# Two token tiles by transposing DMA, a joint first v stage, and a new work order in a fused linear-attention and FFN kernel

## The chip, the cores and the metric

The kernel runs on one core of a Trainium2 chip. The metric is the device time of one execution in microseconds (us); below, "the profiled execution" is a single execution recorded by the hardware profiler, with a record for every instruction of every engine and for the DMA transfers. The engines are PE (matrix multiply), DVE (vector), ACT (scalar, activations), POOL (general) and SP (here it only issues DMAs). PE writes to PSUM, which is used as eight banks in four pairs; DVE and ACT read PSUM, POOL doesn't.

## The reference

For 2048 tokens x of width 640, the output mixes a linear attention A and a gated FFN B with a gate per token:

```python
qkv = x @ wqkv                                   # 32 heads of 20
pq = einsum("bhsd,hdf->bhsf", q, w_phi)
pk = einsum("bhsd,hdf->bhsf", k, w_phi)
phi_q = concat([softmax(pq), softmax(-pq)])      # 40 features per head
phi_k = concat([softmax(pk), softmax(-pk)])
kv = einsum("bhsf,bhsd->bhfd", phi_k, v)
z  = einsum("bhsf->bhf", phi_k)
num = einsum("bhqf,bhfd->bhqd", phi_q, kv)
den = einsum("bhqf,bhf->bhq", phi_q, z)[..., None] + 1e-6
a = (num / den) @ wo
b = (silu(x @ w_gate) * (x @ w_up)) @ w_down     # F = 1728
g = sigmoid((x * gate_w).sum(-1, keepdims=True))
out = g * a + (1 - g) * b
```

All inputs and the output are bfloat16.

## The kernel before

The tokens are 16 tiles of 128 (`NT`), and four blocks of 512 (`NB`) for the FFN. Nothing is scheduled at run time: the string `ORDER` lists short items, and a loop at the end of `_build` emits the instructions of each item in that order. Each engine then runs its own instructions strictly in the order in which they were emitted; a tracker (`_Tracker.run`) adds semaphore waits for data and buffer conflicts. Work thus runs ahead on an engine until an instruction has to wait, and everything behind it on that engine waits too.

The items, with the engines that they use:

- `H` warm-up matmuls of ones (`NWARM` of them each), `G` puts gate_w as a further column into the v weights (`wvg`).
- `X t` transposes token tile t on PE (five 128x128 transposes from `xs`), and DVE copies it to `xT`. Tiles below `NPE` are loaded plainly into `xs` for this; all others are loaded straight into `xT` by a transposing DMA on SP (`load_x`).
- `V t`: v of tile t, ten matmuls of 320 columns into one PSUM pair; ACT copies it to one of six buffers `v1r`, and the gate's column to `svec`.
- `W m`: transposes of a row chunk of wk (from `wkn`), copied by DVE to `wT`; `Y` builds block-diagonal w_phi in `wbd` (two pieces on DVE, three on POOL); `M m` and `R m` multiply wk and wq with it ahead of time (wq is loaded transposed into `wTq`), copied to `wqk` by DVE (even m of `M`) or ACT.
- `K t`: ten matmuls, two exponentials on ACT into one of four `ekr`, sums and reciprocals on DVE, scaling on POOL. `E t`: eleven small matmuls that add tile t to kv in PSUM pair 3. `I` takes that pair out of the ring of pairs (`ring["n"]` from 4 to 3), `N` finishes kv on DVE and gives it back, `Z` broadcasts z.
- `Q t`: ten matmuls, two exponentials on ACT into one of three `eq`. `A t` (qsum), `B t` (qden) and `C t` (qscale) are DVE work of about 1.5, 1.5 and 3 us; `C` ends with a multiplication on POOL into `ph` and a transposing DMA on SP into `phiT`.
- `F b.k`: column chunk k of gate and up for block b: ten matmuls of 512 columns into one pair, tanh and copy on ACT, one DVE operation, one POOL multiplication into `hT`.
- `O b.p`: a third of the attention output of block b, copied by ACT to `oT`. `D b.u`: the last projection of a token tile, 38 matmuls of 320 columns, one scaling on ACT into `osb`, and the store to HBM, issued by SP. The very last tile is done in two halves of 19 matmuls, each with its own ACT operation and store.

Every item that needs PSUM takes the next pair in the ring (`next_pair`), so PE waits where the pair's last user (by four, or between `I` and `N` three, takings ago) has not been read out.

Before the loop, the loads are issued. On ACT's queue: gate_w, wv chunks 0, 2 and 4, x2, w_phi. On SP's queue: x0, wv chunks 1 and 3, x1, x3, five chunks of wk, x4 to x6 by transposing DMA, five chunks of wq by transposing DMA, x7 to x15 by transposing DMA. The item `L` then puts the FFN and output weights behind these on SP's queue.

All matmuls are emitted by the helper at L284, PE transposes by L296, ACT operations by L302, DVE and POOL operations by L308 (copies), L312, L316, L323 and L326, plain DMAs by L338 and transposing ones by L337.

Of the kernel before, what the change touches and what calls it, by code (L numbers as in the profile page):

```python
# [12 lines left out]
NT = S_TOK // P  # L13
NB = 4
NCH = 11
NPE = 4
NV = 6
NWARM = 3
FP = 120 * NCH
FK = FP + 8  # L20
ACTF = mybir.ActivationFunctionType
# [7 lines left out]


ORDER = """
L H0 H1 H2 G H3 H4 H5 X0 H6 H7 V0 X1 X2 X3 V1 Y W0 W1 W2 V2 W3 W4 V3 M0 M1 M2 M3 M4 K0 I V4 K1 R0
K2 V5 K3 E0 R2 V6 K4 E1 K5 R4 E2 K6 E3 V7 K7 R1 E4 V8 E5 K8 K9 V9 F0.0 V10 E6 K10 E7 F0.1 E8 V11
K11 E9 K12 V12 K13 R3 E10 K14 V13 E11 K15 Q0 V14 F0.2 V15 E12 E13 J E14 E15 N Q1 F0.3 Q2 A0 Z A1
B0 A2 F0.4 F0.5 F0.6 C0 B1 F0.7 F1.0 Q3 C1 A3 F0.8 F1.1 B2 F1.2 C2 F0.9 F0.10 B3 Q4 F1.3 A4 Q5 C3
F1.4 F0.11 T F0.12 B4 Q6 C4 A5 F1.5 F1.6 B5 F1.7 O0.0 A6 O0.1 F1.8 B6 Q7 A7 F0.13 O0.2 C5 F1.9
F1.10 Q8 C6 A8 B7 D0.0 D0.1 D0.2 Q9 F1.11 C7 D0.3 F2.0 F2.1 F2.2 F1.12 B8 O1.0 O1.1 O1.2 A9 C8
Q10 F2.3 F1.13 Q11 A10 F2.4 B9 F2.5 C9 A11 B10 Q12 D1.0 F2.6 C10 F2.7 D1.1 F2.8 B11 F2.9 F2.10
Q13 A12 C11 D1.2 Q14 D1.3 O2.0 A13 B12 A14 F3.0 B13 F3.1 F3.2 O2.1 C12 C13 F3.3 F3.4 B14 F2.11
Q15 F2.12 A15 F3.5 F2.13 C14 F3.6 O2.2 B15 F3.7 C15 F3.8 D2.0 F3.9 F3.10 F3.11 F3.12 D2.1 O3.0  # L40
O3.1 O3.2 F3.13 D2.2 D3.0 D3.1 D2.3 D3.2 D3.3
"""


# [143 lines left out]
def _build(nc, A_x, A_wqkv, A_w_phi, A_wo, B_x, B_w_gate, B_w_up, B_w_down, gate_w, out):  # L188
    tr = _Tracker(nc)
    pe, act, dve, pool, sp = nc.tensor, nc.scalar, nc.vector, nc.gpsimd, nc.sync  # L190
# [28 lines left out]
    omg = sb("omg", [P, NT], F32)  # L219
# [37 lines left out]
    wph = at("wph", [P, 5, DH], BF16, 28480)  # L257
# [17 lines left out]
    def mm(pairs):  # L275
        reads, writes = [], []
        for p in pairs:
            reads += [p[1], p[2]]
            writes.append(p[0])

        def fn():
            last = None
            for o, l, r, st, sp_, sk in pairs:
                last = pe.matmul(o, lhsT=l, rhs=r, start=st, stop=sp_, skip_group_check=sk)  # L284
            return last
        return run("pe", fn, list({id(a): a for a in reads}.values()), writes)
# [13 lines left out]
    def actop(o, i, func, scale=1.0):  # L300
        rd = [i] + ([scale] if isinstance(scale, bass.AP) else [])
        return run("act", lambda: act.activation(o, i, func, scale=scale), rd, [o])  # L302

    def copy(e, o, i):
        if e == "act":
            return actop(o, i, ACTF.Copy)
        eo = tr.eng[e]
        return run(e, lambda: eo.tensor_copy(o, i), [i], [o])  # L308
# [23 lines left out]
    def dma(e, dst, src, transpose=False):  # L332
        eo = tr.eng[e]

        def fn():
            if transpose:
                return eo.dma_start_transpose(dst, src)  # L337
            return eo.dma_start(dst, src)  # L338
        rd = [src] if src.tensor.name in tr.base else []
        wr = [dst] if dst.tensor.name in tr.base else []  # L340
        return run(e, fn, rd, wr, dma=True)
# [39 lines left out]
    H0 = [0, 6, 12, 19, 25]  # L381
    H1 = [7, 13, 20, 26, 32]
# [56 lines left out]
    def warm():  # L439

        pr = next_pair()
        mm([(bank(2 * pr, 0, P), ones[:, :], ones[:, :], True, True, False)] * NWARM)

    def vtile(t):
        pr = next_pair()
        pairs = [(bank(2 * pr + hb, 0, 320 + hb), xT[:, t, c, :], wvg[:, c, 320 * hb:640 + hb - 320 * (1 - hb)],
                  c == 0, c == 4, False) for c in range(5) for hb in range(2)]
        if t == 0:
            for c in range(5):
                mm(pairs[2 * c:2 * c + 2])  # L450
        else:
            mm(pairs)
        i = halves(pr).rearrange("p b (h d) -> p b h d", d=DH)
        o = v1v[:, t % NV, 0:H, 0:DH].rearrange("p (b h) d -> p b h d", b=2)
        copy("act", o, i)
        copy("act", svec[:, t:t + 1], bank(2 * pr + 1, 320, 321))

    def head_exps(pr, dst):
        i = halves(pr).rearrange("p b (h d) -> p b h d", d=DH)
        o = dst.rearrange("p (b h s d) -> p b h s d", b=2, s=2, d=DH)  # L460
        actop(o[:, :, :, 0, :], i, ACTF.Exp, 1.0)
        actop(o[:, :, :, 1, :], i, ACTF.Exp, -1.0)
# [183 lines left out]
    out_evs = []  # L646

    def ditem(bt, u):
        buf = bt % 2
        t = 4 * bt + u  # L650
        pr = next_pair()
        tok = slice(P * u, P * u + P)
        ls = [(hT[:, buf, k, tok], wd[:, k, :]) for k in range(13)]
        ls += [(hT[0:104, buf, 13, tok], wd[0:104, 13, :])]
        ls += [(oT[:, buf, m, tok], wog[:, m, :]) for m in range(5)]
        n = len(ls)
        half = [[(bank(2 * pr + hb, 0, 320), l, r[:, 320 * hb:320 * hb + 320], i == 0, i == n - 1, False)
                 for i, (l, r) in enumerate(ls)] for hb in range(2)]
        o = osb[:, t % 4, :]
        if t < NT - 1:  # L660
            mm([p for ab in zip(*half) for p in ab])
            actop(o.rearrange("p (b c) -> p b c", b=2), halves(pr), ACTF.Copy, omg[:, t:t + 1])
            out_evs.append(dma("sp", out2[t * P:(t + 1) * P, :], o))
            return
        for hb in range(2):
            mm(half[hb])
            c = slice(320 * hb, 320 * hb + 320)
            actop(o[:, c], bank(2 * pr + hb, 0, 320), ACTF.Copy, omg[:, t:t + 1])
            out_evs.append(dma("sp", out2[t * P:(t + 1) * P, c], o[:, c]))


    def kv_begin():
# [2 lines left out]
    def kv_end():  # L675
        kv_finish()
        ring["n"] = 4

    ops = {
        "H": lambda i: warm(), "X": xpose, "G": gcol, "V": vtile, "W": wxpose,  # L680
        "M": lambda m: premult(1, m), "R": lambda m: premult(0, m),
        "K": ktile, "E": kvtile, "L": load_ffn_weights, "T": tail_weights, "J": gates,
        "Y": w_blocks, "I": kv_begin, "N": kv_end, "Z": z_broadcast,
        "Q": qtile, "A": qsum, "B": qden, "C": qscale,
        "F": fitem, "O": oitem, "D": ditem,
    }
    for w in ORDER.split():
# [50 lines left out]
```

## Time and profile before

| | |
|---|---|
| median of 4 runs | 295.9 us (295.81 to 296.99) |
| profiled execution, its own time | 295.62 us |
| profiled execution, span from first to last instruction | 293.8 us |
| mean granted TensorE clock | 1.000 |
| DVE, ACT, POOL busy in the span | 171.7, 148.7, 158.0 us |
| DMA moved in the span | 21.28 MB |

The span is shorter than the execution's own time because that has work around the program's first and last instruction. "Busy" of PE counts a matmul from its start to its modelled end, and matmuls overlap, so starts of successive items are a better measure of their cost than the lengths. In the lists of groups, `out<-in` names the tile written and the tiles read; in timelines, a bracket tells how long the engine had been idle and what released it. The costliest groups of PE are the FFN's matmuls of 512 columns (520 of them, mean 379 ns from start to modelled end) and the last projection's of 320 columns (448 with `wd`, mean 299 ns). The page's chain of work that ended last is PE for 90% of the span, DVE for 5% and DMA for 2%.

Some durations that are used below: the DVE reductions of A and C take 1.48 us, the multiplication of B 1.45, the FFN's DVE operation 0.68, its tanh on ACT 0.60 and its copy 0.59; POOL's multiplications take 1.27 (FFN), 2.46 (`ph`) and 2.36 (`ekr`); the two exponentials of a K or Q tile take 1.41 together; a transposing DMA into `phiT` landed 3.5 us after its issue (3.5 to 4.0), one of x 2.9 to 5.5, wk chunks 5.2 to 5.5.

### The profile page before, as it was taken

Reading aid. Unit: us, or ns where it says so; the run is one execution under the profiler, and the core shown is the slowest. Engines: PE = TensorE matmul, PEld = TensorE weight load, DVE = VectorE, ACT = ScalarE, POOL = GpSimd, SP = SyncE. Lnnn points to the kernel's source line nnn. Section 1 sums busy time; section 2 is a strip of 40 time slices with the busy share of each in tenths; the row PEclk is TensorE's granted clock in tenths of the full one; section 3 lists DMA queues with packets and bytes.
Section 4 is the critical chain, followed back from the end, with each engine's and each line's share of the span. In section 5 each row is a group of like instructions: output and inputs, shape, how many; then the busy total and the mean of one; then the engine's idle time right before and its main releaser. Section 6 shows DMA issues by size and latency. Waiting matters only on the chain.

```text
span 293.8 us, 4908 instructions
## 1 busy us (share of the span) xinstructions
PE 288.1 (98%) x1981; PEld 174.2 (59%) x1981; DVE 171.7 (58%) x250; ACT 148.7 (51%) x252; POOL 158.0 (54%) x118
## 2 busy tenths in 40 slices
PE   7999999999999999999999999999999999999996
PEld 5777766766454544457764456647544455657774
DVE  2567874576979989997042777539269893100000
ACT  2278865775746665852235862353356644262112
POOL 8709887794268878855025384544056976410000
PEclk9999999999999999999999999999999999999999
DMA  7968799510002222204203021130302223000101
GB/s 228 197 114 113 213 358 362 116 23 0 2 0 49 51 49 49 49 2 82 63 22 73 3 49 29 44 71 2 94 0 49 51 49 71 3 22 25 45 22 48
DMA packets 45993, 21.28 MB, mean 72 GB/s; under 512 B 35794, under 2 KB 45970, under 8 KB 45970
## 3 DMA queue, kind: packets, MB, share of 16 engines
q1 hardware_dynamic: 44728, 20.27, 29.3%
q10 hardware_dynamic: 1242, 0.68, 0.8%
q8 instruction: 16, 0.26, 0.4%
q14 instruction: 7, 0.06, 0.1%
HBM read 9.78 MB, written 2.62 MB: 42 GB/s over the span
## 4 chain that ended last, share of the span: by engine, by line
PE 90%; DVE 5%; DMA 2%; ACTq 1%; ACT 1%; issue 0%
PE ps L284 90%; DMA xs<-in_A_x_dram 2%; DVE qw L323 1%; DVE hT L316 1%; PE ps L296 1%; ACTq L338 1%; DVE qw L316 1%; DVE qm L583 1%; DVE qz L323 0%; DVE ez L312 0%; ACT hT L302 0%; DVE qd L326 0%; DVE qc L588 0%; DVE qd L312 0%; ACT osb L302 0%
## 5 line engine op out<-in xcount | busy, mean ns | idle before, releaser
L312 POOL TENSOR_TENSOR hT<-hT,us 128x512 bf16<-128x512 bf16 (+1 forms) x56 | 69.8, 1259 | 62.5 <-DVE hT L316 62.4
L316 DVE SCALAR_TENSOR_TENSOR hT<-hT,ps 128x512 bf16<-128x512 bf16 (+1 forms) x56 | 37.6, 682 | 61.7 <-ACT hT L302 51.0
L284 PE MATMUL ps<-xT,wg 128*128 128x512 bf16 x260 | 64.6, 379 | 0.3 <-DVE hT L316 0.2
L284 PE MATMUL ps<-xT,wu 128*128 128x512 bf16 x260 | 64.6, 379 | 0.0
L284 PE MATMUL ps<-wd,hT 128*128 128x320 bf16 x448 | 63.7, 299 | 0.0
L302 ACT ACTIVATE hT<-ps 128x512 bf16<-128x512 f32 (+2 forms) x60 | 35.8, 596 | 47.0 <-PE ps L284 45.1
L284 PEld LDWEIGHTS ps<-wd,hT 128*128 128x128 bf16 x448 | 43.8, 98 | 17.8
L312 POOL TENSOR_TENSOR ph<-eq,qc 128x1320 bf16<-128x1320 bf16 x16 | 39.3, 2457 | 27.1 <-DVE qc L588 27.1
L284 PE MATMUL ps<-wqk,xT 128*128 128x320 bf16 x320 | 48.4, 299 | 0.1
L312 POOL TENSOR_TENSOR ekr<-ekr,krec 128x1280 bf16<-128x1280 bf16 x16 | 37.3, 2357 | 15.7 <-DVE krec L326 13.5
L284 PEld LDWEIGHTS ps<-xT,wu 128*128 128x128 bf16 x260 | 25.4, 98 | 30.7
L302 ACT ACTIVATE osb<-ps,omg 128x640 bf16<-128x640 f32 (+1 forms) x17 | 13.0, 762 | 58.5 <-PE ps L284 58.5
L284 PEld LDWEIGHTS ps<-xT,wg 128*128 128x128 bf16 x260 | 24.9, 98 | 29.5 <-issue 1.2
L284 PEld LDWEIGHTS ps<-wqk,xT 128*128 128x128 bf16 x320 | 30.4, 98 | 14.0 <-ACT us L302 0.5
L302 ACT ACTIVATE us<-ps 128x512 bf16<-128x512 f32 (+1 forms) x56 | 33.2, 593 | 0.6 <-POOL hT L312 0.5
L323 DVE TENSOR_REDUCE ksum<-ekr 128x64 f32<-128x1280 bf16 x16 | 23.5, 1468 | 14.7 <-ACT ekr L302 14.7
L302 ACT ACTIVATE eq<-ps 128x640 bf16<-128x640 f32 x32 | 22.5, 704 | 15.7 <-POOL ph L312 11.3
L302 ACT ACTIVATE ekr<-ps 128x640 bf16<-128x640 f32 x32 | 22.5, 704 | 8.4 <-PE ps L284 7.9
L284 PE MATMUL ps<-wvg,xT 128*128 128x320 bf16 (+1 forms) x160 | 24.8, 300 | 0.2 <-DMA wvg<-in_A_wqkv_dram 0.2
L284 PE MATMUL ps<-wog,oT 128*128 128x320 bf16 x160 | 24.5, 299 | 0.0
L323 DVE TENSOR_REDUCE qz<-eq 128x64 f32<-128x1280 bf16 x16 | 23.6, 1479 | 1.3 <-ACT eq L302 1.3
L323 DVE TENSOR_REDUCE qw<-ez 128x64 f32<-128x1280 bf16 x16 | 23.6, 1477 | 0.0
(71 smaller groups left out, 196.2 us busy)
## 6 DMA issues: line engine op xcount, KB each, us to landing
out_dram<-osb SPq DMA_DIRECT2D x15, 160.0 KB, 1.8
wd<-in_B_w_down_dram SPq DMA_DIRECT2D x1, 2080.0 KB, 16.6
wkn<-in_A_wqkv_dram SPq DMA_DIRECT2D x5, 160.0 KB, 5.4
wg<-in_B_w_gate_dram SPq DMA_DIRECT2D x1, 800.0 KB, 9.7
wu<-in_B_w_up_dram SPq DMA_DIRECT2D x1, 800.0 KB, 11.3
wog<-in_A_wo_dram SPq DMA_DIRECT2D x2, 375.0 KB, 6.6
wg<-in_B_w_gate_dram SPq DMA_DIRECT2D x1, 720.0 KB, 12.1
wu<-in_B_w_up_dram SPq DMA_DIRECT2D x1, 720.0 KB, 12.5
```

What stands on the lines that cost most here:

```text
L284: last = pe.matmul(o, lhsT=l, rhs=r, start=st, stop=sp_, skip_group_check=sk)
L296: last = pe.transpose(o, i, ident[0:k, 0:k])
L302: return run("act", lambda: act.activation(o, i, func, scale=scale), rd, [o])
L312: return run(e, lambda: eo.tensor_tensor(o, a, b, op), [a, b], [o])
L316: return run("dve", lambda: dve.scalar_tensor_tensor(out=o, in0=a, scalar=s, in1=b, op0=op0, op1=op1), rd, [o])
L323: return run("dve", lambda: dve.tensor_reduce(o, i, AX.X, ALU.add), [i], [o])
L338: return eo.dma_start(dst, src)
L583: run("dve", lambda: dve.tensor_tensor(v2(qm[:, s, :]), v2(qw[:, s, :]), qs, ALU.mult), [qw[:, s, :], qz[:, b, :]], [qm[:, s, :]])
```

## The change

- `NPE` goes from 4 to 2: tiles 2 and 3 are no longer loaded into `xs` and transposed on PE; they come by transposing DMA on SP like tiles 4 to 15.
- The loads are dealt out anew: x1 goes on ACT's queue ahead of its wv chunks; wv chunks 0, 2, 4 go on SP and 1, 3 on ACT; x2 and x3 by transposing DMA stand on SP behind the wv chunks and ahead of the five wk chunks.
- `U` (`vfirst`) replaces V0 and V1: it takes two PSUM pairs and runs both tiles chunk by chunk of wv; both are copied out afterwards.
- The second half of the last tile is stored by a DMA that ACT issues; the first half still by SP.
- `NWARM` is 4, with six `H` items ahead of everything instead of eight of 3 spread out.
- `ORDER` is another one throughout. The O items of a block now stand closer together, `I` stands before W4 instead of after K0, and the places of F, Q, A, B, C and D items among each other differ everywhere.

```diff
-NPE = 4
+NPE = 2
-NWARM = 3
+NWARM = 4
...
-L H0 H1 H2 G H3 H4 H5 X0 H6 H7 V0 X1 X2 X3 V1 Y W0 W1 W2 V2 W3 W4 V3 M0 M1 M2 M3 M4 K0 I V4 K1 R0
+H2 H0 H3 H1 L H5 H4 G X0 X1 U V2 W0 W1 Y V3 W2 W3 I W4 M2 M1 M0 M4 M3 K0 K1 K2 V4 K3 V5 R0 E0 V6
...
-B0 A2 F0.4 F0.5 F0.6 C0 B1 F0.7 F1.0 Q3 C1 A3 F0.8 F1.1 B2 F1.2 C2 F0.9 F0.10 B3 Q4 F1.3 A4 Q5 C3
-F1.4 F0.11 T F0.12 B4 Q6 C4 A5 F1.5 F1.6 B5 F1.7 O0.0 A6 O0.1 F1.8 B6 Q7 A7 F0.13 O0.2 C5 F1.9
...
-Q13 A12 C11 D1.2 Q14 D1.3 O2.0 A13 B12 A14 F3.0 B13 F3.1 F3.2 O2.1 C12 C13 F3.3 F3.4 B14 F2.11
-Q15 F2.12 A15 F3.5 F2.13 C14 F3.6 O2.2 B15 F3.7 C15 F3.8 D2.0 F3.9 F3.10 F3.11 F3.12 D2.1 O3.0
-O3.1 O3.2 F3.13 D2.2 D3.0 D3.1 D2.3 D3.2 D3.3
...
+F1.7 F0.11 A4 F1.8 Q5 Q6 F0.12 F0.13 F1.9 F1.10 A5 O0.0 B4 O0.1 O0.2 F1.11 B5 F1.12 C4 A6 Q7 B6
+D0.0 C5 A7 Q8 C6 D0.1 D0.2 B7 Q9 C7 A8 F1.13 D0.3 Q10 A9 B8 F2.0 C8 A10 O1.0 O1.1 B9 O1.2 F2.1
+F2.2 C9 Q11 B10 C10 D1.0 F2.3 Q12 A11 B11 D1.1 D1.2 Q13 F2.4 F2.5 A12 A13 F2.6 F2.7 F2.8 C11 F2.9
...
+F3.5 B15 F3.6 O2.1 O2.2 F3.7 F3.8 C14 D2.0 F3.9 D2.1 C15 F3.10 F3.11 F3.12 O3.0 O3.1 O3.2 F3.13
+D2.2 D2.3 D3.0 D3.1 D3.2 D3.3
...
     load_x(0)
+    load_x(1, "act")
     for c in range(5):
-        load_rows("sp" if c % 2 else "act", wvg[:, c, 0:D], c, 2 * D)
-    load_x(1)
-    load_x(2, "act")
+        load_rows("act" if c % 2 else "sp", wvg[:, c, 0:D], c, 2 * D)
+    load_x(2)
+    dma("act", wph[:, :, :], A_w_phi.rearrange("h e f -> (h e) f").rearrange("(c p) f -> p c f", p=P))
     load_x(3)
-    dma("act", wph[:, :, :], A_w_phi.rearrange("h e f -> (h e) f").rearrange("(c p) f -> p c f", p=P))
...
+    def vfirst():
+
+        prs = [next_pair(), next_pair()]
+        pairs = [v_pairs(t, prs[t]) for t in range(2)]
+        for c in range(5):
+            for t in range(2):
+                mm(pairs[t][2 * c:2 * c + 2])
+        for t in range(2):
+            v_out(t, prs[t])
...
-        for hb in range(2):
-            mm(half[hb])
-            c = slice(320 * hb, 320 * hb + 320)
-            actop(o[:, c], bank(2 * pr + hb, 0, 320), ACTF.Copy, omg[:, t:t + 1])
-            out_evs.append(dma("sp", out2[t * P:(t + 1) * P, c], o[:, c]))
+        mm(half[0])
+        actop(o[:, 0:320], bank(2 * pr, 0, 320), ACTF.Copy, omg[:, t:t + 1])
+        out_evs.append(dma("sp", out2[t * P:(t + 1) * P, 0:320], o[:, 0:320]))
+        mm(half[1])
+        actop(o[:, 320:D], bank(2 * pr + 1, 0, 320), ACTF.Copy, omg[:, t:t + 1])
+        out_evs.append(dma("act", out2[t * P:(t + 1) * P, 320:D], o[:, 320:D]))
```

`v_pairs` and `v_out` are the two halves of the old `vtile`: the ten matmuls of a tile, and ACT's two copies.

More of the change, by code (lines that the diff above doesn't have):

```diff
@@ L31 @@
 ORDER = """
-L H0 H1 H2 G H3 H4 H5 X0 H6 H7 V0 X1 X2 X3 V1 Y W0 W1 W2 V2 W3 W4 V3 M0 M1 M2 M3 M4 K0 I V4 K1 R0
-K2 V5 K3 E0 R2 V6 K4 E1 K5 R4 E2 K6 E3 V7 K7 R1 E4 V8 E5 K8 K9 V9 F0.0 V10 E6 K10 E7 F0.1 E8 V11
-K11 E9 K12 V12 K13 R3 E10 K14 V13 E11 K15 Q0 V14 F0.2 V15 E12 E13 J E14 E15 N Q1 F0.3 Q2 A0 Z A1
-B0 A2 F0.4 F0.5 F0.6 C0 B1 F0.7 F1.0 Q3 C1 A3 F0.8 F1.1 B2 F1.2 C2 F0.9 F0.10 B3 Q4 F1.3 A4 Q5 C3
-F1.4 F0.11 T F0.12 B4 Q6 C4 A5 F1.5 F1.6 B5 F1.7 O0.0 A6 O0.1 F1.8 B6 Q7 A7 F0.13 O0.2 C5 F1.9
-F1.10 Q8 C6 A8 B7 D0.0 D0.1 D0.2 Q9 F1.11 C7 D0.3 F2.0 F2.1 F2.2 F1.12 B8 O1.0 O1.1 O1.2 A9 C8
-Q10 F2.3 F1.13 Q11 A10 F2.4 B9 F2.5 C9 A11 B10 Q12 D1.0 F2.6 C10 F2.7 D1.1 F2.8 B11 F2.9 F2.10
-Q13 A12 C11 D1.2 Q14 D1.3 O2.0 A13 B12 A14 F3.0 B13 F3.1 F3.2 O2.1 C12 C13 F3.3 F3.4 B14 F2.11
-Q15 F2.12 A15 F3.5 F2.13 C14 F3.6 O2.2 B15 F3.7 C15 F3.8 D2.0 F3.9 F3.10 F3.11 F3.12 D2.1 O3.0
-O3.1 O3.2 F3.13 D2.2 D3.0 D3.1 D2.3 D3.2 D3.3
+H2 H0 H3 H1 L H5 H4 G X0 X1 U V2 W0 W1 Y V3 W2 W3 I W4 M2 M1 M0 M4 M3 K0 K1 K2 V4 K3 V5 R0 E0 V6
+E1 K4 V7 K5 R1 E2 K6 E3 V8 K7 V9 E4 V10 E5 K8 K9 E6 V11 E7 R3 K10 K11 R2 E8 F0.0 E9 V12 K12 K13
+F0.1 E10 V13 K14 E11 R4 F0.2 K15 V14 Q0 A0 V15 E12 F0.3 E13 E14 E15 N F1.0 Q1 A1 Z B0 F0.4 J Q2
+C0 F1.1 B1 F1.2 C1 F1.3 F0.5 A2 Q3 F0.6 F0.7 A3 B2 F0.8 F1.4 F0.9 B3 Q4 F0.10 T C2 F1.5 F1.6 C3
+F1.7 F0.11 A4 F1.8 Q5 Q6 F0.12 F0.13 F1.9 F1.10 A5 O0.0 B4 O0.1 O0.2 F1.11 B5 F1.12 C4 A6 Q7 B6
+D0.0 C5 A7 Q8 C6 D0.1 D0.2 B7 Q9 C7 A8 F1.13 D0.3 Q10 A9 B8 F2.0 C8 A10 O1.0 O1.1 B9 O1.2 F2.1
+F2.2 C9 Q11 B10 C10 D1.0 F2.3 Q12 A11 B11 D1.1 D1.2 Q13 F2.4 F2.5 A12 A13 F2.6 F2.7 F2.8 C11 F2.9
+D1.3 B12 C12 F2.10 F3.0 F2.11 B13 Q14 A14 F3.1 Q15 A15 F3.2 F2.12 B14 F3.3 O2.0 C13 F2.13 F3.4
+F3.5 B15 F3.6 O2.1 O2.2 F3.7 F3.8 C14 D2.0 F3.9 D2.1 C15 F3.10 F3.11 F3.12 O3.0 O3.1 O3.2 F3.13
+D2.2 D2.3 D3.0 D3.1 D3.2 D3.3
 """
@@ L442, in warm, with v_pairs, v_out @@
         mm([(bank(2 * pr, 0, P), ones[:, :], ones[:, :], True, True, False)] * NWARM)
[L444 to L452, printed above, removed]
+    def v_pairs(t, pr):
+        return [(bank(2 * pr + hb, 0, 320 + hb), xT[:, t, c, :], wvg[:, c, 320 * hb:640 + hb - 320 * (1 - hb)],
+                 c == 0, c == 4, False) for c in range(5) for hb in range(2)]
+    def v_out(t, pr):
         i = halves(pr).rearrange("p b (h d) -> p b h d", d=DH)
@@ L456, in vtile @@
         copy("act", svec[:, t:t + 1], bank(2 * pr + 1, 320, 321))
+    def vtile(t):
+        pr = next_pair()
+        mm(v_pairs(t, pr))
+        v_out(t, pr)
+    def vfirst():
[6 more added lines that the diff above has]
+            v_out(t, prs[t])
     def head_exps(pr, dst):
@@ L679, in _build @@
     ops = {
-        "H": lambda i: warm(), "X": xpose, "G": gcol, "V": vtile, "W": wxpose,
+        "H": lambda i: warm(), "X": xpose, "G": gcol, "U": vfirst, "V": vtile, "W": wxpose,
         "M": lambda m: premult(1, m), "R": lambda m: premult(0, m),
```

## The prediction

> **What bounds the kernel now.** I read the page first: the span, the busy times and the slices.
>
> ```profile
> span 293.8 us, 4908 instructions
> PE 288.1 (98%) x1981; PEld 174.2 (59%) x1981; DVE 171.7 (58%) x250; ACT 148.7 (51%) x252; POOL 158.0 (54%) x118
> PE   7999999999999999999999999999999999999996
> ```
>
> TensorE is busy for 288.1 of 293.8 us and only its first and last slices are not full. Nothing done to another engine can bring anything unless PE starts its dense stretch earlier, has less to do, stops less often on the way, or the tail behind it shrinks. 293.8 - 288.1 = 5.7 us is all the idle time there is. The list of PE's waits says where it lies:
>
> ```profile
> PE ps L284 <- DVE ones L330: 1.1, 1, 1.1
> PE ps L296 <- DMA xs<-in_A_x_dram: 0.9, 1, 0.9
> PE ps L284 <- DVE hT L316: 0.5, 2, 0.3
> ```
>
> 1.1 us is start-up, 0.9 us is the wait for x2 and x3, 0.5 us are two stops in the middle; 2.5 us more lie behind the last matmul. So I went to the timeline of PE's first 18 us, which the change rewrites (columns: start, length, engine):
>
> ```profile
> 4.20 0.85 PE L284 MATMUL ps<-ones 128*128 128x128 bf16 x6
> 5.00 1.29 PE L284 MATMUL ps<-wvg,xT 128*128 128x320 bf16 x8
> ...
> 6.73 0.44 PE L296 MATMUL ps<-ident,xs 128*128 128x128 bf16 x5
> 8.04 0.73 PE L296 MATMUL ps<-ident,xs 128*128 128x128 bf16 x10 [0.87 <-DMA xs<-in_A_x_dram]
> 8.61 1.54 PE L284 MATMUL ps<-wvg,xT 128*128 128x320 bf16 x10
> 9.99 1.00 PE L296 MATMUL ps<-ident,wkn 128*128 128x128 bf16 x15
> ```
>
> V0 begins at 5.00, X1 sits at 6.73, X2 and X3 come at 8.04 after the wait, V1 at 8.61. Starts give prices: a V tile 9.99 - 8.61 = 1.38 us (0.138 per matmul), a W item 1.02 / 3 = 0.34. The other engines' rows around it show what feeds this stretch and what ends it:
>
> ```profile
> 3.15 2.33 SPq L338 DMA_DIRECT2D wkn<-in_A_wqkv_dram  x5
> 5.52 4.70 SPq L337 DMA_TRANSPOSE xT<-in_A_x_dram  x3
> 11.45 1.27 POOL L312 TENSOR_TENSOR wbd<-wph,bmask 128x160 bf16<-128x160 bf16 x3
> 14.85 2.29 DVE L308 CAST wqk<-ps 128x640 bf16<-128x640 f32 x3 [1.08 <-PE ps L284]
> 17.19 0.11 PEld L284 LDWEIGHTS ps<-wqk,xT 128*128 128x128 bf16 x2 [0.22 <-DVE wqk L308]
> ```
>
> K0's last pair of matmuls waits for the third cast of wqk, so the preamble ends at 17.47, where the timeline has V4's first matmul. From there PE is dense. The point to forecast is when K0 ends in the new order, since both kernels have then done V0 to V3, all W and M items and K0.
>
> **The change, part by part: the front.** Removed are X2 and X3: ten transposes and two DVE copies; on PE they take 8.61 - 8.04 = 0.57 us, and the 0.87 us wait before them goes as a wait for a plain load. Warm-up stays at 24 matmuls (8x3 then, 6x4 now); back to back, at 0.103 each (9 from 2.74 to 3.67), they end near 3.6, so X0 stays where it was, at 3.67. X1 is new at this place: x1 is ACT's second issue at 1.41; ACT's issue at that time landed 2.9 us later, at 4.3. X1 then runs 4.3 to 4.8, its copy (0.49) ends near 5.45. U's first two matmuls go at 4.99, the rest from 5.45: 18 x 0.138 = 2.48, end 7.93. Its last chunk, c4, is the seventh load, as many as had landed before at 6.38 (issued 2.28, 4.1 to landing); U needs it at 7.4, a cover of 1 us. So V0 and V1 are done at 7.93, where before V1 ended at 9.99.
>
> V2 runs 7.93 to 9.31. x2 by transpose is SP's fifth issue, at about 2.65 (0.81, then four of 0.40 to 0.46). Transposes landed 2.9 to 5.5 us after issue, so by 8.15 at the latest: at worst 0.2 us late. x3 follows 1.3 to 2.2 us later, by 10.35 at worst; V3 wants it at 10.4.
>
> Now what is queued behind: wkn's five issues stand behind both transposes on SP. Three transposes took 4.70 us of SP, two take 3.1 to 3.4, so wkn starts near 6.0 instead of 3.15; x4 to x6, wTq, x7 to x15 and the FFN weights move back by 2.4 us (two transposes in, two plain issues out). Those later ones have cover: V4 runs after 19 us and x4 lands near 14; V7 runs near 27 and x7, issued near 20.7, lands by 24.4 (3.6); FFN weights are first used beyond 45 us and land about 42. wkn has little. Windows of the trace give the DMA price:
>
> ```profile
> 5.00:8.00 3.00, 2.01 (x16) 1.13 (x15) 0.49 (x1) 0.78 (x3) 3.00 (x5) 1.00 1.07 317
> 20.00:30.00 10.00, 10.00 (x101) 7.42 (x100) 7.37 (x9) 8.14 (x14) 8.26 (x4) 1.00 0.79 115
> ```
>
> The last two columns are the DMA engines' share and GB/s. Saturated with mostly plain loads they move 317 GB/s, 164 KB in 0.52 us; in a stretch of transposes alone 115 / 0.79 = 146 GB/s, 1.12 us. Two transposes add 1.2 us ahead of wkn. wkn0 landed at 3.15 + 5.2 = 8.35; I take 9.55, and 10.1 for wkn1. The bounds: issue at 6.0 plus 2.3 (the first load, alone) is 8.3; plus 5.5 (wkn's longest) is 11.5.
>
> By the Trainium skill ("Advanced Engine Details and Errata", section X-Bar Transpose (TRN2)), transposing DMAs on this chip are as fast as regular ones; these windows do not bear that out. By that rule wkn0 would still land at 8.35 and the front gain would be that of the fast rival below.
>
> With 9.55: W0 9.55 to 9.89, W1 10.1 to 10.44, V3 10.44 to 11.82, W2 and W3 to 12.5. With I moved ahead, the ring has three pairs here, and counting next_pair calls W4 takes V3's pair: V3's two ACT copies end about 12.8 (in the old run 0.81 after V3's modelled end), so W4 runs 12.82 to 13.16. wbd on POOL is ready at 12.72, as before, and no longer matters. M2, M1, M0 follow at 0.34 each (30 matmuls 14.33 to 16.05) to 14.2; M4 reuses M2's pair and waits for its cast until 14.6; M3 ends 15.3. Casts on DVE: 13.8, 14.6, 15.35 to 16.1; ACT's copy of M3 ends 16.17. K0's chunks 3 and 4 then take 4 x 0.138: K0 ends at 16.75 against 17.47. **Gain 0.7 us**, though V0 and V1 were 2 us early: the rest is spent on wkn, the pair of W4 and the cast chain.
>
> The warm-up is also weighed against a rule. Rows: six 128-column matmuls at 4.20 took 0.80 to the next start, eight of 320 columns from 5.00 only 1.29, so the clock was up by 5.00. The Trainium skill ("TensorE: Matmul & The Clock Gate", Part 1) says the activity window runs free and the change point varies between runs. By its rule a late opening could make part of U run at half speed, some 2 us by my estimate; by the row, nothing, since PE is now busier before 5.00.
>
> **The middle.** The order from K0 to D3.3 is rewritten, with the same items. Summing rows (V, K, Q 1.38, F 2.16, D 38 x 0.137 = 5.2) PE's work there is equal. Both stops of 0.5 us in all stood where DVE was behind, the first in this window:
>
> ```profile
> 110.00:120.00 10.00, 9.63 (x50) 4.10 (x49) 9.79 (x12) 6.83 (x11) 8.90 (x9) 1.00 0.22 43
> 117.97 0.62 PE L284 MATMUL ps<-phiT,kvsb 120*64 120x512 bf16 x4 [0.31 <-DVE hT L316]
> ```
>
> DVE is at 9.79 of 10. Setting DVE work (A 1.48, B 1.45, C 3.1, F 0.68) against PE's time item by item, the old order has 5.3 us queued on DVE at C4 A5 and 6.7 at C12 C13, each with F items and short O items behind. In the new order C4 A6 Q7 B6 also leave 5.3, and C10 leaves 8.3, but a D of 5.2 us of pure PE work follows each. I count the two stops as gone: **gain 0.5 us**, bounds 0 (they come back elsewhere) to 0.7 (every stop gone). Where ACT is held (Q7's exps wait for POOL's ph of tile 4), F1.12 to those exps is 0.60 + 0.68 + 3.1 + 2.46 + 1.41 = 8.2 us, and PE wants that pair only after Q7 D0.0 Q8 D0.1, 13 us. C15 stands late: from F3.9, 0.15 + 0.60 + 0.68 + 3.1 + 2.46 + 3.5 (transpose landing) = 10.5 us against 11.7 us of D2.1 and three F before O3.0. Cover 1.2 us; landings reach 4.0, a DVE step of 0.23 can take 1.09, so at worst 0.2 us is lost.
>
> **The tail.** The last half is issued by ACT after its own copy instead of SP: an issue took 0.45 on ACT at the start, 0.40 on SP, landing 1.6. I put this at 0, bounds -0.1 to +0.1.
>
> **The sum.** 0.7 + 0.5 = 1.2 us. The profiled execution took 295.62 us, 1.8 around its span; its span becomes 292.6 and its time 294.4. The median, 295.9, is 0.3 above it: I forecast 294.7 us, with its own range 294.1 to 295.2.
>
> **Rivals.**
> 1. DVE's stops come back at other places, and only the front's 0.7 stays: 295.2. For it: DVE is at nine tenths from 70 to 130 us in either order, and 8.3 us at C10 is more than the old order ever queued. Against it: the D items behind.
> 2. Slower: wkn comes late. SP's transposes hold it and DMA is saturated, as when it took 5.5 us: landing at 11.5 moves W0 by 1.95 us and K0's end to 18.7, 1.2 later than before; with the middle's gain 296.6, without it 297.1. It decides from a landing of 10.3 (front gain gone); from 11.2 on the kernel is slower by more than the gain of the middle hides. Against it: the DMA engines have less to move before it than when it took 5.5 us.
> 3. Faster: the transposes cost the loads nothing, wkn0 lands by 9.3. Then W0 9.31, V3 ends 11.4, W4 goes at 12.4, M2 at 12.75 (wbd on POOL), K0 ends 16.35: 1.1 + 0.5 gives 294.3.
>
> **How the numbers follow.** Forecast 0.52, rival 1 0.22, rival 2 0.17, rival 3 0.09. About 0.3% (0.9 us) is what a measurement of this kernel can tell from no change: faster means below 295.0. Forecast mostly (0.44), rival 3 whole and a little of rival 1 (0.04) give 0.57 faster; the rest of these two gives about 0.24 within it, rival 2 with an unnamed stop 0.19 slower. The range runs from below rival 3 (293.9) to the better half of rival 2, 296.4.
>
> **What would show it.** U from 5.0 to 7.9 without a wait over 0.5 us; no PE wait on xT; W0 at 9.3 to 9.8; K0's end at 16.4 to 17.0; PE waits on DVE under 0.3 us in all; 2.5 us behind the last matmul. A wait for wkn above 0.8 us, matmuls of U spaced 0.26 us, or more than 0.5 us of new stops between 20 and 290 us would make it wrong.

## The result, and the profile after

The changed kernel takes 294.58 us (median of 45 runs, 293.83 to 297.56); the kernel before took 295.94 us in the runs beside it. The ratio is 0.9951, with a 95% interval of 0.9941 to 0.9961: faster by 1.2 to 1.7 us. The forecast was 294.7 us, with a span of 292.6 us for the profiled execution; this is the page of the changed kernel.

```profile
span 292.6 us, 4885 instructions
PE 286.5 (98%) x1971; PEld 173.9 (59%) x1971; DVE 167.9 (57%) x248; ACT 148.6 (51%) x252; POOL 157.6 (54%) x118
PE   7999999999999999999999999999999999999996
```

PE is still the bound, has ten instructions fewer, and ends 1.2 us earlier. The list of what PE waited for (time in total, times, longest) is no shorter than before:

```profile
...
PE ps L296 <- DMA xs<-in_A_x_dram: 0.7, 1, 0.7
PE ps L284 <- DVE kvsb L312: 0.6, 1, 0.6
PE ps L296 <- ACT svec L302: 0.3, 1, 0.3
PE ps L284 <- DVE xT L308: 0.3, 1, 0.3
PE ps L284 <- DVE wqk L308: 0.3, 1, 0.3
```

So new stops took the place of old ones, and a sum has to be made by place. The timeline of PE's front in the changed kernel (start, length, what):

```profile
3.91 0.45 PE L296 MATMUL ps<-ident,xs 128*128 128x128 bf16 x5
5.07 0.45 PE L296 MATMUL ps<-ident,xs 128*128 128x128 bf16 x5 [0.70 <-DMA xs<-in_A_x_dram]
5.36 0.44 PE L284 MATMUL ps<-wvg,xT 128*128 128x320 bf16 x2
6.11 4.02 PE L284 MATMUL ps<-wvg,xT 128*128 128x320 bf16 x28 [0.32 <-DVE xT L308]
9.97 0.72 PE L296 MATMUL ps<-ident,wkn 128*128 128x128 bf16 x10
...
12.95 0.44 PE L296 MATMUL ps<-ident,wkn 128*128 128x128 bf16 x5 [0.33 <-ACT svec L302]
...
14.74 0.80 PE L284 MATMUL ps<-wbd,wT 128*128 128x140 bf16 x12 [0.27 <-DVE wqk L308]
15.47 4.30 PE L284 MATMUL ps<-wqk,xT 128*128 128x320 bf16 x30
```

K0 begins at 15.47, and the eleventh matmul of its row, the first of K1, starts at 16.89. Before, the matmul behind K0 started at 17.47: the front is 0.58 us shorter. (The expectations below give K0's end as 16.85, ten steps of 0.138; one of the steps is 0.178.) The last ACT operation of the program waits for the last matmul. The first line is the kernel before, the second the changed one:

```profile
291.33 0.53 ACT L302 ACTIVATE osb<-ps,omg 128x320 bf16<-128x320 f32 x1 [2.06 <-PE ps L284]
```

```profile
290.09 0.53 ACT L302 ACTIVATE osb<-ps,omg 128x320 bf16<-128x320 f32 x1 [2.06 <-PE ps L284]
```

It starts 1.24 us earlier. The stretch from K0's end to there is therefore 273.20 us instead of 273.85: another 0.65 us shorter, with the same items in it. From this operation's start to the end of the span nothing changed: 2.5 us in both.

What became of the middle can be read from starts of matmuls. (A stop is longer than the idle time that a list of waits gives, because the modelled ends of matmuls reach over the start of the next: a group of 320 columns runs at 0.136 per matmul but is drawn 0.30 long.) Three things add up:

- The old order's stops for DVE near 117 and 225 us are gone: 0.45 and 0.39 us by the starts, and two of 0.15 and 0.11. The second, in the kernel before:

```profile
224.28 1.52 PE L284 MATMUL ps<-wqk,xT 128*128 128x320 bf16 x10
226.03 1.24 PE L284 MATMUL ps<-xT,wg 128*128 128x512 bf16 x5 [0.23 <-DVE hT L316]
```

- The O parts stand together. Each run of them costs PE something on the way in and out. The first two lines are O2.0 in the kernel before, the others O0 and O2.0 in the changed one.

```profile
210.10 0.62 PE L284 MATMUL ps<-phiT,kvsb 120*64 120x512 bf16 x4
210.66 1.25 PE L284 MATMUL ps<-xT,wg 128*128 128x512 bf16 x5
```

```profile
123.53 1.24 PE L284 MATMUL ps<-xT,wu 128*128 128x512 bf16 x5
124.71 1.49 PE L284 MATMUL ps<-phiT,kvsb 120*64 120x512 bf16 x11
126.28 1.24 PE L284 MATMUL ps<-xT,wg 128*128 128x512 bf16 x5
...
223.66 0.62 PE L284 MATMUL ps<-phiT,kvsb 120*64 120x512 bf16 x4
224.22 1.25 PE L284 MATMUL ps<-xT,wt 128*128 128x512 bf16 x5
```

A part of four matmuls alone holds PE for 0.56 us, a whole block of eleven for 1.57. The five matmuls ahead of the run take 1.18 from start to start instead of 5 x 0.216 = 1.08: 0.1 us more on the way in. Seven runs became five; summed over all of them, with the stop of 0.45 taken out, O items cost 0.31 us less.
- A new stop stands before Z. The timeline of the changed kernel around it:

```profile
71.77 2.20 DVE L312 TENSOR_TENSOR dz<-ident,zf 120x1320 bf16<-120x1320 bf16 x1
73.89 1.15 DVE L312 TENSOR_TENSOR kvsb<-ps,hmask 120x160 bf16<-120x160 f32 x6
75.10 0.73 PE L284 MATMUL ps<-dz,ones 120*128 120x480 bf16 x3 [0.56 <-DVE kvsb L312]
```

Z needs only `dz`, ready at 73.97, before Q1's matmuls end. But the pair that it takes from the ring is pair 3, just given back by `N`, and DVE's six `kvsb` operations still read it until 75.04. Z starts 0.72 us late, and 0.07 us more are lost behind it. The sum is 0.45 + 0.39 + 0.26 + 0.31 - 0.79 = 0.62 us, of the 0.65 measured.

In the old order Z takes pair 3 too, without a stop. Q1, F0.3 and Q2 stand between `N` and Z there, 1.4 us more of PE's time than F1.0 and Q1. And `dz` takes less of DVE's; in the kernel before it is

```profile
70.66 1.53 DVE L312 TENSOR_TENSOR dz<-ident,zf 120x1320 bf16<-120x1320 bf16 x1
```

while POOL is idle. In the changed kernel it takes 2.20 us, and POOL multiplies beside its first 0.8 us:

```profile
71.42 1.16 POOL L312 TENSOR_TENSOR hT<-hT,us 128x512 bf16<-128x512 bf16 x1 [1.97 <-DVE hT L316]
```

It is the same in all profiles: 1.53 us with the old order behind K0 (two profiles), 2.2 with the new one (twelve). The difference, 0.67 us, is nearly the whole stop. No experiment moved POOL's operation alone, so that it is the reason is not shown.

### The profile page after: what moved, and what is told of

The parts are those of the page before. It is cut to its first block, busy times and chain, and to the rows that moved or that the text cites. A ratio compares the mean times of both kernels' runs of the same rounds, so it can differ in the third digit from the quotient of the medians.

```text
span 292.6 us, 4885 instructions
## 1 busy us (share of the span) xinstructions
PE 286.5 (98%) x1971; PEld 173.9 (59%) x1971; DVE 167.9 (57%) x248; ACT 148.6 (51%) x252; POOL 157.6 (54%) x118
## 4 chain that ended last, share of the span: by engine, by line
PE 95%; DVE 2%; DMA 1%; ACT 1%; issue 0%; ACTq 0%
PE ps L284 94%; DMA xs<-in_A_x_dram 1%; DVE dz L312 1%; PE ps L296 1%; DVE kvsb L312 0%; DVE wqk L308 0%; ACT v1r L302 0%; DVE hT L316 0%; ACT hT L302 0%; ACTq L338 0%; ACT osb L302 0%; DVE xT L308 0%; DVE wT L308 0%; DVE zf L323 0%; DVE zt L312 0%
## 5 line engine op out<-in xcount | busy, mean ns | idle before, releaser
L312 POOL TENSOR_TENSOR hT<-hT,us 128x512 bf16<-128x512 bf16 (+1 forms) x56 | 68.4, 1232 | 60.6 <-DVE hT L316 56.5
L284 PE MATMUL ps<-wqk,xT 128*128 128x320 bf16 x320 | 47.8, 299 | 0.0
```

Source lines behind the costliest of these rows:

```text
L312: return run(e, lambda: eo.tensor_tensor(o, a, b, op), [a, b], [o])
```

## The experiments

Each kernel was timed in turn with the kernel before. Medians of the kernel before lay between 295.70 and 295.86 us in these runs. The experiments have twelve runs each, V0 by chunks and three stops out six. The profile is of one execution, so what depends on landing times in it is a sample of one.

| kernel | median us | ratio to before, 95% | span of the profile |
|---|---|---|---|
| changed kernel | 294.58 | 0.9951 [0.9941, 0.9961] | 292.6 |
| front alone | 294.77 | 0.9967 [0.9955, 0.9978] | 292.7 |
| rest of the order alone | 295.30 | 0.9983 [0.9970, 0.9996] | 293.3 |
| last store by SP | 294.29 | 0.9961 [0.9938, 0.9983] | 292.6 |
| V0 and V1 apart, in batches | 297.49 | 1.0046 [1.0018, 1.0074] | 294.9 |
| x1 first | 294.65 | 0.9975 [0.9954, 0.9996] | 292.8 |
| Z later | 293.95 | 0.9947 [0.9930, 0.9963] | 294.0 |
| O parts split | 295.32 | 0.9996 [0.9980, 1.0012] | 293.9 |
| V0 by chunks, then V1 | 294.75 | 0.9966 [0.9953, 0.9979] | 292.8 |
| I behind K0 | 294.85 | 0.9964 [0.9942, 0.9986] | 294.5 |
| x2, x3 on PE | 295.40 | 0.9983 [0.9965, 1.0002] | 294.4 |
| warm-up between X0 and X1 | 294.39 | 0.9954 [0.9934, 0.9975] | 293.3 |
| three stops out | 293.60 | 0.9920 [0.9899, 0.9942] | 291.9 |

**1. The front and the rest, each alone.**

```diff
 the changed loads and order up to K0, then:
-K1 K2 V4 K3 V5 R0 E0 V6 E1 K4 V7 ...
+V4 K1 R0 K2 V5 K3 E0 R2 V6 K4 E1 ...
```

> The changed loads, warm-up and order up to K0, then the old order from V4 on (without I, which already stands ahead), last half stored by SP. Theory (the two gains add): K0's ten matmuls end at 16.85 us as in the changed kernel against 17.47 before, and the old order's stops behind it (0.45 us at the O part near 117, 0.39 us near 225) stay: 0.6 us faster than before, about 295.3. Rival (the front's gain is spent again later, because DVE or POOL bounds the rest): K0's end moves, the time does not, 295.9 +- 0.2.

```diff
 the old loads and order up to K0 and I, then:
-V4 K1 R0 K2 V5 K3 E0 R2 V6 K4 E1 ...
+K1 K2 V4 K3 V5 R0 E0 V6 E1 K4 V7 ...
```

> The old loads, warm-up and order up to K0 and I, then the changed order from K1 on, last half stored by SP. Theory: K0 ends at 17.47 as before; the old stops near 117 and 225 are gone, Z waits some 0.7 us for DVE's kvsb, five runs of O parts instead of seven save 0.3 us: 0.6 us faster, about 295.3. Rival (the changed order is worth something only behind the earlier front): 295.9 +- 0.2. Rival (all of the gain is the order): 294.6.

The front alone brings 1.1 us, the rest alone 0.6; the whole 1.4. The gains add within the intervals (0.7 to 1.3, 0.1 to 0.9, and 1.2 to 1.7), so neither rival holds. In the profile of the front alone, V4 stands at the place that K0's end sets:

```profile
15.05 1.58 PE L284 MATMUL ps<-wqk,xT 128*128 128x320 bf16 x10
16.47 1.54 PE L284 MATMUL ps<-wvg,xT 128*128 128x320 bf16 x10
```

16.47 against 17.47 before, and the last ACT operation at 290.31 against 291.33: the front's gain of 1.0 arrives at the end undiminished. It is 0.4 more than in the changed kernel's own profile: x1 landed at 4.44 us here and at 5.02 there, with the same instructions ahead of it. The stretch from K0's end to the last ACT operation is 273.85 us with the old order and this front, as in the kernel before. In the rest alone it is 273.19, as in the changed kernel. So the middle's 0.65 us comes with the order and does not depend on the front.

In the rest alone the stop stands elsewhere:

```profile
71.40 0.69 DVE L316 SCALAR_TENSOR_TENSOR hT<-hT,ps 128x512 bf16<-128x512 bf16 x1 [1.55 <-ACT hT L302]
72.24 1.24 PE L284 MATMUL ps<-xT,wg 128*128 128x512 bf16 x5 [0.46 <-DVE zt L312]
...
75.85 0.73 PE L284 MATMUL ps<-dz,ones 120*128 120x480 bf16 x3
```

The older front took a different number of pairs, so at `N` the ring hands F1.0 pair 1, the one that F0.3 just ahead of it has used. PE waits 0.62 us by the starts until DVE has read F0.3's result (the list names DVE's next operation, `zt`, which reads pair 3). Z takes pair 3 here too, but later, and waits only 0.1 us.

**2. The last store.**

```diff
-        out_evs.append(dma("act", out2[t * P:(t + 1) * P, 320:D], o[:, 320:D]))
+        out_evs.append(dma("sp", out2[t * P:(t + 1) * P, 320:D], o[:, 320:D]))
```

> The changed kernel with the second half of the last tile stored by SP again. Theory: no difference, from the last matmul's start to the end of the span within 0.1 us of the changed kernel's, time 294.6 +- 0.2. Rival (SP's queue is held by the first half's store): 0.3 to 0.5 us longer behind the last matmul.

Both spans are 292.6 us; from the start of the last ACT operation to the end it is 2.4 us with SP and 2.5 with ACT. The store's queue makes no difference that can be measured.

**3. U taken apart.**

```diff
-... G X0 X1 U V2 W0 ...
+... G X0 X1 V0 V1 V2 W0 ...
```

> The changed kernel with U taken apart: V0, then V1, each tile's ten matmuls in one batch with nothing of the other between. Theory (the wait inside U is for x1 and its copy, the wv chunks have all but landed): V0 starts near 5.4 to 6.2 when its last chunk lands, V1 ends at 8.1 to 9.0; M2 can't start before wbd is ready near 12.95, so K0 ends 0 to 0.4 us earlier than 16.85: 294.2 to 294.6. Rival (running the two tiles together is what hides the chunks' landing): V0 waits, V1 ends 0.5 us or more after the 8.59 of the changed kernel, and K0 ends at 17.2 or later: 295.0.

The theory missed by 3 us. PE's timeline in that profile:

```profile
3.91 1.38 PE L296 MATMUL ps<-ident,xs 128*128 128x128 bf16 x10
6.78 5.61 PE L284 MATMUL ps<-wvg,xT 128*128 128x320 bf16 x30 [1.48 <-DMA wvg<-in_A_wqkv_dram]
```

Two losses are in these lines. V0 in one batch waits for the last wv chunk, which landed at 6.53, and starts at 6.78, where U started at 5.36. And 30 matmuls take 5.61 us, where 28 took 4.02: the first ten are spaced 0.268 us, the rest 0.139. So TensorE ran at half its pace until 9.4 us. The trace's record of the granted clock begins at 9.53 us in this profile and at 3.91 in the changed kernel's, each time where the spacing halves. Ahead of it there is no entry, and the views print full speed. A second form, with V0 fed chunk by chunk, takes out the wait:

```diff
     def vtile(t):
         pr = next_pair()
-        mm(v_pairs(t, pr))
+        pairs = v_pairs(t, pr)
+        if t == 0:
+            for c in range(5):
+                mm(pairs[2 * c:2 * c + 2])
+        else:
+            mm(pairs)
```

> The changed kernel with U taken apart again, but V0 fed chunk by chunk as in the kernel before, V1 in one batch behind it. Theory (what the run with both in batches lost is the wait for the last wv chunk and the clock that then opens late; the joint order of the two tiles itself brings nothing): V0 starts near 5.3, V1 ends at 8.1 to 8.6, the clock is up as in the changed kernel, K0's end within 0.4 us of 16.85: 294.2 to 294.8. Rival (the two tiles interleaved are what covers the chunks' landing): V0 waits 0.4 us or more for a chunk and V1 ends past 9.0: 295.0 to 295.4.

V1 ends at 8.58 us, U ended at 8.59. V0 waits for a chunk once, for about 0.24 us, U for x1's copy. The two ends can't be compared closely: x1 landed 0.6 us earlier here (4.43), and the clock came up at 6.0 instead of 3.9. The medians can: 294.75 and 294.58. Feeding chunk by chunk is what counts, 2.7 us in the median; interleaving the two tiles brings nothing that these runs can tell. How much of the 2.7 us is the wait and how much the late clock stays open: the runs with both tiles in batches lie between 295.3 and 299.6.

**4. x1 first.**

```diff
-    dma("act", gwr[0:5, :], ...)
     load_x(0)
     load_x(1, "act")
+    dma("act", gwr[0:5, :], ...)
```

(The kernel issues x1, then gate_w on ACT, then x0 on SP.)

> The changed kernel with x1 issued first on ACT's queue and gate_w second. Theory (the front waits for x1's landing, which came at 5.03 us in one profile and at 4.44 in another): x1 lands by 4.0, X1 follows X0, U's later matmuls start near 5.3, and the end of K0 moves from 16.85 to 16.4, not further, because M2 then waits for wbd on POOL near 12.9: median 0.3 to 0.4 us under the changed kernel, 294.2. Rival (x1's landing is set by what else the DMA engines move, not by its place): lands at 4.4 to 5.0 again, no difference, 294.6.

x1 lands at 3.9 us and X1 follows X0 without a stop, yet W0 starts at 9.95 us, as in the changed kernel (9.97). U now waits for a wv chunk instead, its matmuls run without a gap only from 6.35 us on. The rival is wrong on x1's landing and right on the time: in this profile the stop only moved from x1 to a wv chunk.

**5. x2 and x3 on PE.**

```diff
-NPE = 2
+NPE = 4
-... X0 X1 U V2 W0 ...
+... X0 X1 U X2 X3 V2 W0 ...
```

> The changed kernel with x2 and x3 loaded plainly at the same places of SP's queue and transposed on PE between U and V2, in PSUM pairs 3 and 0. Theory (the transposing DMA is worth PE's ten transposes, 0.56 us, and nothing else): everything from V2 on 0.6 us later, 295.2. Rival 1 (DVE's copies and V2's wait for them cost more): 295.5. Rival 2 (the plain loads are so much quicker for the DMA engines, or the waits for V3's pair so long, that the transposes hide): 294.6.

```profile
7.14 2.37 PE L284 MATMUL ps<-wvg,xT 128*128 128x320 bf16 x16 [0.71 <-DMA wvg<-in_A_wqkv_dram]
9.35 0.72 PE L296 MATMUL ps<-ident,xs 128*128 128x128 bf16 x10
10.38 1.55 PE L284 MATMUL ps<-wvg,xT 128*128 128x320 bf16 x10 [0.31 <-DVE xT L308]
```

V2 starts at 10.38 instead of 8.59: U ends 0.76 later because it waits for wv, the transposes take 0.57, and V2 waits 0.47 (by the starts) for DVE's copy. In the median it is 0.8 us slower than the changed kernel, nearest to the first rival: the transposes and V2's wait for the copy, 1.04 us together, account for it. The wait for wv is a surprise, but this execution took 296.10 us, the longest of its twelve, and the median has no room for it. In this execution the last two wv chunks took 5.6 and 5.7 us to land, against 4.2 and 4.5 with the transposes. With plain loads, x3 is issued 0.9 and wkn 1.7 us earlier, since a transposing DMA occupies SP for 1.3 us and a plain one for 0.43. Whether these loads held the wv chunks up is not shown: with the kernel before's loads, x2, x3 and wkn plain too, the last chunk landed 4.1 us after its issue in one profile and 5.0 in another.

**6. Z later.**

```diff
     def kv_end():
         kv_finish()
-        ring["n"] = 4
+    def pair_back():
+        k = ring["i"]
+        ring["o"] = [3] + [(k + j) % 3 for j in range(3)]
+        ring["n"], ring["i"] = 4, 0
...
-N F1.0 Q1 A1 Z B0 F0.4 J
+N F1.0 Q1 A1 F0.4 P Z B0 J
```

(`next_pair` takes its pair from the list `ring["o"]`; `P` is `pair_back`.)

> The changed kernel with Z behind F0.4, and PSUM pair 3 given back only just ahead of Z, so that Z takes it, and not the first item that needs a pair. Theory (the changed order's one long stop, 0.72 us before Z and 0.22 behind it, is the wait for DVE to read kv out of pair 3, and nothing else is late there): both stops go, the rest keeps its pace: 0.7 to 0.9 us under the changed kernel, 293.8. Rival (DVE is behind anyway, B0 and C0 come later by as much, and PE stops at a later F item instead): 294.4 to 294.8.

The median is 293.95, 0.63 below the changed kernel's. The timeline of that profile has Z without a wait, and one new stop further on:

```profile
77.26 1.24 PE L284 MATMUL ps<-xT,wu 128*128 128x512 bf16 x5
78.34 0.72 PE L284 MATMUL ps<-dz,ones 120*128 120x480 bf16 x3
...
92.82 1.25 PE L284 MATMUL ps<-xT,wg 128*128 128x512 bf16 x5 [0.25 <-DVE hT L316]
```

By the starts, 0.79 us are gained at Z and 0.41 lost near 92 us, where DVE is late: 0.38 us in this profile. The rest of the 0.63 is not accounted for. Both theories are partly right: what one stop gives back, a busy DVE takes in part. (That profile's span of 294.0 is among the longest of its runs, most of which are near 292.1: the first 14 matmuls of U and those of X0 and X1 ran at half the pace.)

**7. O parts split.**

```diff
-O0.0 B4 O0.1 O0.2 F1.11 B5        -O1.0 O1.1 B9 O1.2 F2.1
+O0.0 B4 F1.11 O0.1 O0.2 B5        +O1.0 F2.1 O1.1 B9 O1.2
-O2.1 O2.2 F3.7                    -O3.0 O3.1 O3.2 F3.13
+O2.1 F3.7 O2.2                    +O3.0 F3.13 O3.1 O3.2
```

> The changed kernel with one F item put between two O parts in each of the four blocks: nine runs of O parts instead of five, nothing else moved but B4 and B9. Theory (every run of O parts costs PE about 0.14 us on the way in and out, whoever is behind it): 4 x 0.14 = 0.56 us slower than the changed kernel, 295.1, and the starts of the matmuls show 0.09 us extra into each run. Rival (the O parts gained only because the old order's stop at 117 us went): no difference, 294.6 +- 0.2.

295.32 us, 0.74 slower than the changed kernel. By the starts, the four splits cost 0.41 us: 0.07 each in the blocks where four and seven matmuls take the place of eleven, 0.22 where a part of three is cut off. The extra on the way into each run is 0.09 us, as expected. Another 0.43 us is a stop that the edit itself made, at Q11:

```profile
163.30 1.06 PE L284 MATMUL ps<-phiT,kvsb 120*64 120x512 bf16 x7
...
166.89 1.38 PE L284 MATMUL ps<-wqk,xT 128*128 128x320 bf16 x9 [0.27 <-DVE hT L316]
```

So a run of O parts has a price of its own, 0.10 us in the mean of the four, under the 0.14 us that I had put in.

**8. I behind K0.**

```diff
-... V3 W2 W3 I W4 M2 M1 M0 M4 M3 K0 K1 ...
+... V3 W2 W3 W4 M2 M1 M0 M4 M3 K0 I K1 ...
```

> The changed kernel with I moved back behind K0, so that W4 and the M items use four PSUM pairs. Theory (the prediction's: the front loses 0.33 us where W4 takes V3's pair and 0.27 where M4 waits for M2's cast, because the ring has three pairs): both waits go, M2 starts near 12.95 (wbd on POOL), K0 ends near 16.5 instead of 16.85, 0.3 us under the changed kernel, 294.3. Rival (the cast chain on DVE ends when it did, so K0 only waits inside itself): K0 ends at 16.8, no difference, 294.6.

```profile
5.71 6.52 PE L284 MATMUL ps<-wvg,xT 128*128 128x320 bf16 x30
...
14.01 1.00 PE L296 MATMUL ps<-ident,wkn 128*128 128x128 bf16 x15
15.12 1.93 PE L284 MATMUL ps<-wbd,wT 128*128 128x140 bf16 x30
17.30 2.89 PE L284 MATMUL ps<-wqk,xT 128*128 128x320 bf16 x20 [0.24 <-DVE wqk L308]
```

The waits of W4 and M4 are gone: the 15 transposes run through, and the 30 M matmuls but for 0.19 us. K0 now waits for the cast chain before it starts. From W0's start to K0's end it is 6.6 us against 6.9, so 0.3 us are gained at the place. The median, 294.85, doesn't show it, and neither does this execution, the longest of its twelve: 30 matmuls take 6.52 us here, since the clock came up at 10 us. Runs of this kernel lie between 293.8 and 296.4.

**9. Warm-up between X0 and X1.**

```diff
-H2 H0 H3 H1 L H5 H4 G X0 X1 U
+H2 H0 H3 H1 L G X0 H5 H4 X1 U
```

> The changed kernel with the last two of the six warm-up items between X0 and X1 instead of ahead of X0: as much PE work, but PE does not sit idle while x1 lands. Theory (the profiles whose clock opened late, at 6.9 and 9.5 us, are those with PE idle between X0 and X1 or before U; kept busy, it opens by 5.2): U's matmuls at 0.139 from the start, no run above 295.5, median 0 to 0.3 us under the changed kernel. Rival (the late opening is chance, whatever PE does): runs above 296 as often as in the changed kernel, 5 of 45.

(Of the changed kernel's 45 runs, 3 were above 296 us, not 5.) The timeline lists no idle time of PE from 2.9 us on, and yet:

```profile
4.49 0.74 PE L296 MATMUL ps<-ident,xs 128*128 128x128 bf16 x5
5.03 5.59 PE L284 MATMUL ps<-wvg,xT 128*128 128x320 bf16 x30
```

Eight matmuls are spaced 0.268 us, the clock comes up at 7.4, and one of 12 runs took 296.5. The theory falls: keeping PE busy does not make the clock open by 5.2 us. Whether it excludes the openings near 10 us, three of which were seen and all behind idle time of PE, stays open; an idle time of 0.2 us at the same place also went with openings at 5.2 and 5.4 (last store by SP, three stops out).

**10. Three stops out.** Z later, I behind K0, and one more: in six of the profiles PE waited 0.2 to 0.4 us (by the starts) for the last transpose of `phiT` before O3.0.

```diff
-D2.0 F3.9 D2.1 C15 F3.10
+D2.0 C15 F3.9 D2.1 F3.10
```

> The changed kernel with three of the stops taken out: Z behind F0.4 with pair 3 given back late (as in the run that moved Z), I behind K0 (as in the run that moved I), and C15 ahead of F3.9 instead of behind D2.1, so that O3.0 no longer waits for its transpose (0.3 to 0.5 us in five of the profiles). Theory (the three are at places that don't touch each other): 0.65 (Z) + 0.25 (I) + 0.1 to 0.3 (C15) under the changed kernel, 293.5, and the profile shows no wait of PE on phiT, none on svec in the front and none on kvsb. Rival (the gain of one is spent at the next place where DVE is late, as 0.4 us was near 92 us when Z was moved): 293.9 to 294.3, with stops of 0.4 us or more between 80 and 130 us.

293.60 us, 0.9920 [0.9899, 0.9942]: faster than the kernel before by 2.2 us, and about 1.0 below the changed kernel. PE's waits for DVE in its profile:

```profile
PE ps L284 <- DVE xT L308: 0.3, 1, 0.3
...
PE ps L284 <- DVE hT L316: 0.2, 1, 0.2
PE ps L284 <- DVE wqk L308: 0.2, 1, 0.2
```

No wait on phiT, kvsb or svec is left. The theory's sum (293.5) is met to 0.1 us, by six runs. Its first term is not: the stop of 0.41 us near 90 us, which the rival named, stays, and the profile's stretch behind K0 is 0.38 us shorter than the changed kernel's, not 0.65. In front of it moving I gives 0.32 us (K0's end at 16.57 instead of 16.89). The transpose of C15 cost the changed kernel's own profile nothing, so the rest of the 1.0 us can't be read from this pair of profiles.

## Why the prediction was right, point by point

- *Front, 0.7 us:* 0.58 in the profile, 1.0 in that of the front alone. The sum held, three of its terms did not. x1 landed 3.6 us after its issue, at 5.02 instead of 4.3, so U ended at 8.59 instead of 7.93. wkn0 landed 3.5 us after its issue, at 8.83, and not at 9.55: the price that I took from the windows of saturated DMA did not hold, and SP issued the two transposes in 2.64 us, not 3.1 to 3.4. W0 waited for PE, not for wkn. The two errors nearly cancel, and that is luck. The ring of three pairs (0.33 at W4, 0.27 at M4) was as forecast, and moving I shows it.
- *The transposes' cover.* V2 and V3 did not wait for x2 and x3, as forecast. That they save the wait for DVE's copies too, 0.47 us where x2 and x3 stand on PE, I had not counted.
- *Rule and row.* The statement of the Trainium skill ("Advanced Engine Details and Errata", X-Bar Transpose) that transposing DMAs are as fast as regular ones did not decide anything here: by it wkn0 would land at 8.35, by the row at 9.55; it landed at 8.83, and W0 started at 9.97, behind V2.
- *Middle, 0.5 us:* measured 0.65, by other parts. The two stops went (0.84 by their starts, not 0.5: I had taken idle times for stops). I had none in their place, and there is one of 0.72 at Z; my check of DVE's backlog looked at the queue's length and not at which pair the next item takes. It also took one duration for each DVE operation, where `dz` takes 1.53 or 2.20 us, and the 1.45 of B is a mean of 0.81 to 2.67. And I priced the O parts at nothing, which were 0.31, and two small stops, which were 0.26.
- *The signs that I had named.* K0's end (16.89) and the 2.5 us behind the last matmul came as said. W0 started at 9.97, outside 9.3 to 9.8. PE's waits for DVE are 1.2 us in the list instead of under 0.3, and one of them, for x1's copy, is on xT, where I had excluded any. And the new stop of 0.79 us between 20 and 290 us is above the 0.5 that by my own words would make the prediction wrong. So the mechanism of the middle was wrong, and its number is luck: 0.91 us of gains that I did not count, against 0.79 of a stop that I did not see.
- *C15's cover.* Forecast 1.2 us, at worst 0.2 lost. The last transpose took 4.3 us to land in the changed kernel's profile and up to 5.1 in others; 0.6 us of cover was left, and up to 0.41 us was lost in others.
- *Tail, 0:* confirmed.
- *Clock.* The row said nothing would happen, and in the changed kernel's profile nothing did (X0 at 56 ns per matmul from 3.9 us). In others something did: the clock came up at 3.9, 5, 7.4, 9.5 and 10 us in different profiles, and the latest opening cost 1.9 us (15 matmuls at 0.267 us instead of 0.138), near the 2 us that I had estimated. The Trainium skill ("TensorE: Matmul & The Clock Gate", Part 1) says that the window runs free and the point varies between runs. The runs agree that it varies, by 6 us and not by the half microsecond either way that the page gives. Whether the longest runs of each kernel are late openings is not shown, since each kernel has one trace.
- *Rivals.* DVE's stops did come back at another place (rival 1), but for less than went. wkn late (rival 2) did not happen, though rival 3's early landing did (8.83); its gain was used up by x1. (Rival 2's second threshold should be a landing of 10.8 by its own terms, 10.3 and the middle's 0.5, not 11.2.)

## What to carry to other kernels

When a kernel's bound engine is busy 98% of the time, make the sum by place from starts of its instructions, not from lists of waits: the 1.2 us here are six terms of both signs. Before moving an item to the point where a buffer comes back into a ring, ask who takes it next, whether it has been read out, and how long the reader takes with its neighbours busy. And where two terms of a forecast rest on one guess about landing times, check them by a run in which only that load moves: here both were wrong and cancelled.

## What the runs showed of the hardware

- A run of matmuls that write half of the PSUM partitions (120x512 by 64 columns, in pairs that start 0.004 us apart) cost PE 0.09 us on the way in, for every run in these profiles. Cutting a run in two cost 0.07 us in three places and 0.22 in a fourth.
- DVE's `dz` multiplication took 1.53 us with POOL idle and 2.20 with a POOL multiplication beside its first 0.8 us.
- The clock of TensorE came up anywhere from 3.9 to 10 us after the start with the same warm-up, while the row of granted clock stood at full speed throughout. The spacing of matmuls shows it (0.268 against 0.139 us for 320 columns), and in nine of the fourteen traces the clock's record begins only there.
- x1's landing with the same queues ahead of it varied from 2.9 to 3.75 us after its issue between eleven executions, and the last phiT transpose, behind two stores, from 3.5 to 5.1, where the median transpose took 3.5.
